# Who asks for which weight blocks: eight blocks of the last batch by SyncE instead of GpSimd, two blocks of the first routed task by GpSimd instead of SyncE

## The chip, the core and the metric

The kernel runs on one core of a Trainium2 chip. The core has TensorE (PE in the profile, with its weight loads as PEld), VectorE (DVE), ScalarE (ACT), GpSimd (POOL) and SyncE (SP), which run their own instruction queues and wait for each other by semaphores. Sixteen DMA engines move data between HBM and the on-chip memory SBUF; SyncE and ScalarE ask for plain transfers, GpSimd for gathers by a list of row numbers. The metric is the device time of one execution in microseconds (us), the median of several runs.

## What is computed

The reference chains three layers. Attention runs over 4 batches of 8 heads, 1152 keys and 576 pooled queries, and its 2304 output rows of 512 numbers go through a routed mixture of eight experts and then through a soft one:

```
x = attention(q, k, v)                  # 2304 rows of 512
logits = x @ w_gate + modality_bias[modality_id]
e_idx = argmax(logits, axis=1)
for e in range(8):
    mask = e_idx == e
    h = maximum(x[mask] @ w1[e], 0)     # 512 -> 1024
    out[mask] = gate_w[mask] * (h @ w2[e])
# third layer: 32 slots, softmax over rows, eight experts on four slots each
return (softmax(logits2, 1) @ slot_out)
```

Which rows go to which expert is known only while the kernel runs, so the weights of an expert are fetched by an index that the kernel has computed.

## The kernel before, in words

**Attention.** `attention` walks over 16 pairs (batch, two heads), p = 0 to 15. In each pair 36 positions follow each other; at a position TensorE makes scores (lines 266 and 272), ScalarE their exponentials (`e`, line 276), TensorE the product with V (line 286), VectorE the row maxima for the next pair (line 219) and GpSimd the sums of the exponentials (`acc`, lines 297 and 299). Other work is hung on positions by tables of numbers. In the middle pairs SyncE loads a later pair; from p = 13 on no pair is left to load.

**The task ahead.** At the end of batch 2 the kernel picks the expert with most rows so far (`Ahead.select`; its index list is `awidx`, line 1036, one column for each quarter of w1 and w2, row e x 128 + partition). A first task for this expert, the "task ahead", is prepared while the last batch is still in attention, in memory that attention no longer needs (`KX`, `QX`, one `V`). `Ahead.fetch(i)`, line 1047, brings its eight weight blocks of 128 x 1024 floats (512 KB): four of w1, then four of w2. Two are fetched in p = 13, four in p = 14, at positions 1, 5, 21 and 25, and two at the start of p = 15. `Ahead.split(u)` cuts half a block into a high and a low part (ScalarE line 796, VectorE line 797): blocks 0 to 2 during p = 14 and 3 to 5 during p = 15, the rest behind attention. `Ahead.load_x` gathers the task's 256 rows in p = 15.

**The routed tasks.** Behind attention `make_tasks` finds, on VectorE, which expert each of eight static tasks has (`widx`, line 758) and which rows (`xidx`, line 739). `ffn`, inside it `chain`, runs these tasks (t = 0 to 7, and a half task). Each has eight blocks; for t = 0 the order is (w1, quarter 0), (w2, 0), (w1, 1), (w2, 1), and so on. `fetch` in `chain` (line 1187) has SyncE read the expert's row number from `widx` into a register and then asks for a block at that address; since the rows of one quarter of one expert lie one behind the other, that is one plain transfer. Four buffers take the blocks (`RAWS`). At the start the loop of line 1214 asks for four blocks; ahead of block number `min(BX, NRAW - 1)`, which is 3, it puts `load_x(ts[0])`, the gather of task 0's 256 rows in two halves of 128 x 520 floats (`xg`, line 1109, by GpSimd through `gather`, line 775).

**The seam.** Behind that loop come, in program order, four splits (the fourth cuts the first half of block (w1, 1), the third one asked for), and `xT`: TensorE turns the rows (line 784, tile `tp`), ScalarE copies the high part (`xh`, line 791) and VectorE takes the low part (`xl`, line 792). TensorE does the last units of the task ahead (lines 819 to 821) in between. The first product of task 0 is line 805 (`xh`), the second line 806 (`xl`). Each engine keeps its program order, so what stands ahead of `xh` on ScalarE has to be done first.

Of the kernel before, what the change touches and what calls it, by code (L numbers as in the profile page):

```python
# [25 lines left out]
E = 8  # L26
# [51 lines left out]
OUTB = ((6, 6, 6), (8, 10), (2, 4, 4, 8))  # L78
NRAW = sum(RAWS)
BT = 6  # L80
BX = 3
BS = (1, 3)
NHI = 5
NH = 2
# [689 lines left out]
def gather(nc, out, src, idx):  # L774
    return nc.gpsimd.indirect_dma_start(out=out, out_offset=None, in_=src,  # L775
                                        in_offset=bass.IndirectOffsetOnAxis(ap=idx, axis=0))
# [18 lines left out]
def cut_parts(nc, hi, lo, x):  # L795
    nc.scalar.copy(hi, x)  # L796
    nc.vector.tensor_sub(lo, x, hi.bitcast(F32))  # L797


def ffn1(nc, g, wh, wl, xh, xl):  # L800

    hp = g["ps"].tile([128, 512], F32, name="hp", tag="sc", bufs=3)[:, :TS]
    for k in range(DM // 128):
        c = slice(k * 128, (k + 1) * 128)
        nc.tensor.matmul(hp, wh[:, c], xh[:, k], start=(k == 0), stop=False)  # L805
        nc.tensor.matmul(hp, wh[:, c], xl[:, k], start=False, stop=False)  # L806
        nc.tensor.matmul(hp, wl[:, c], xh[:, k], start=False, stop=(k == DM // 128 - 1))  # L807
    return hp


def relu_parts(nc, hp, hh, hl):
    nc.scalar.activation(hh, hp, AF.Relu)  # L812
    nc.vector.scalar_tensor_tensor(out=hl, in0=hp, scalar=0.0, in1=hh.bitcast(F32), op0=ALU.max, op1=ALU.subtract)  # L813


def ffn2(nc, yp, f, hh, hl, wh, wl):
    for h in range(2):
        hs = slice(h * 128, (h + 1) * 128)
        nc.tensor.matmul(yp[h], hh[:, hs], wh, start=(f == 0), stop=False)  # L819
        nc.tensor.matmul(yp[h], hh[:, hs], wl, start=False, stop=False)  # L820
        nc.tensor.matmul(yp[h], hl[:, hs], wh, start=False, stop=(f == F // 128 - 1))  # L821
# [159 lines left out]
class Ahead:  # L981
# [62 lines left out]
        ]  # L1044

    def fetch(self, i):
        gather(self.tc.nc, self.raw[i], self.g["w1" if i < 4 else "w2"], self.widx[:, i % 4:i % 4 + 1])

    def load_x(self, h):
        gather(self.tc.nc, self.xg[h], self.g["xs"][0:PAD + (B - 1) * SQ, :], self.xidx[:, h:h + 1])  # L1050
# [33 lines left out]
def ffn(ctx, tc, g):  # L1084
    nc = tc.nc
# [19 lines left out]
    def load_x(t, xg=None):  # L1105
        halves = 1 if t == HT else 2
        xg = xg or [xp1.tile([128, XW], F32, name=f"xg{h}") for h in range(halves)]
        for h in range(halves):
            gather(nc, xg[h], g["xs"], g["xidx"][:, h, t:t + 1])
        st[t] = dict(xg=xg, gt=xp.tile([128, 2], F32, name="gt"))  # L1110

    def xT(t):
        s = st[t]
        xh = xp1.tile([128, KD, TS], F32R, name="xh")
        xl = xp1.tile([128, KD, TS], F32R, name="xl")
        s["xh"], s["xl"] = xh, xl
        if t == HT:
            nc.gpsimd.tensor_copy(s["gt"][:, 0:1], s["xg"][0][:, DM:DM + 1])
            tp = ps.tile([128, KD, 128], F32, name="tp", tag="mx", bufs=3)
            for k in range(KD):  # L1120
                nc.tensor.transpose(tp[:, k], s["xg"][0][:, k * 128:(k + 1) * 128], ident)
            cut_parts(nc, xh[:, :, 0:128], xl[:, :, 0:128], tp)
            return
        for h in range(2):
            nc.gpsimd.tensor_copy(s["gt"][:, h:h + 1], s["xg"][h][:, DM:DM + 1])
        for a in range(KD // 2):
            k2 = slice(2 * a, 2 * a + 2)
            turn_rows(nc, g, s["xg"], a, xh[:, k2], xl[:, k2])
# [38 lines left out]
    def chain(ts, hooks, between=lambda: False):  # L1167

        seq = []
        for t in ts:  # L1170
            if t == HT:
                seq += [(t, w, f) for w, f0, n in ((1, 0, 4), (2, 0, 2), (1, 4, 2), (2, 2, 2), (1, 6, 2), (2, 4, 4)) for f in range(f0, f0 + n)]
                continue
            seq += [(t, 1, 0)] + [x for f in range(1, 8) for x in ((t, 1, f), (t, 2, f - 1))] + [(t, 2, 7)]
        pieces = sorted({(t, w, f // 2) for t, w, f in seq}, key=lambda x: seq.index((x[0], x[1], 2 * x[2])))
        raw, part, used, row = {}, {}, set(), {}
        left = [len(RAWS)]

        def fetch():
            if pieces:  # L1180
                t, w, q = pieces.pop(0)
                m = len(pieces) % NRAW
                i = next(i for i in range(len(RAWS)) if m < sum(RAWS[:i + 1]))
                raw[t, w, q] = raws[i].tile([128, 1024], F32, name="wraw", bufs=RAWS[i])
                if t not in row:
                    row[t] = nc.sync.value_load(g["widx"][0:1, 0, t:t + 1], min_val=0, max_val=(E - 1) * 128)
                nc.sync.dma_start(out=raw[t, w, q], in_=g[f"w{w}"][bass.ds(row[t] + q * E * 128, 128), :])

        def split(i):
            if i < len(seq):  # L1190
                t, w, f = seq[i]
                x = raw[t, w, f // 2]
                if (t, w) == (HT, 2):
                    part[t, w, f] = x, None
                    return
                part[t, w, f] = hi, lo = g["parts"]()
                if (t, w) == (HT, 1):
                    cut_parts(nc, four(hi), four(lo), x.rearrange("p (f k c) -> p f k c", f=2, k=KD)[:, :, f % 2 * 2:f % 2 * 2 + 2])
                else:
                    cut_parts(nc, hi, lo, x[:, (f % 2) * 512:(f % 2 + 1) * 512])  # L1200
                if f % 2:
                    done(t, w, f)

        def done(t, w, f):
            used.add((t, w, f // 2))
            while raw and next(iter(raw)) in used:
                raw.pop(next(iter(raw)))
                fetch()
                while left[0] and len(raw) <= sum(RAWS[:left[0] - 1]):
                    left[0] -= 1  # L1210
                    cs[left[0]].close()
                    open_more(NWR[left[0]])

        for i in range(NRAW):
            if i == min(BX, NRAW - 1):
                load_x(ts[0])
            fetch()
        for _ in range(BT):
            between()
        for i in range(NHI - 1):  # L1220
            split(i)
            if i in BS:
                between()
        xT(ts[0])
        while between():
            pass
        for i, (t, w, f) in enumerate(seq):
            s = st[t]
            nx = ts[ts.index(t) + 1] if t != ts[-1] else None
            hi, lo = part.pop((t, w, f))  # L1230
            if t == HT:
                half(s, w, f, hi, lo)
                if w == 2 and f % 2:
                    done(t, w, f)
                if (w, f) == (1, 0):
                    load_x(nx)
                if (w, f) == (1, 7):
                    xT(nx)
                if (w, f) == (2, 7):
                    todo.extend([None] + front.put([s["yp"]], s["gt"], [g["xidx"][:, 0, t:t + 1]], t))  # L1240
                    todo.extend(front.group())
                    st.pop(t)
            elif w == 1:
                hp = ffn1(nc, g, hi, lo, s["xh"], s["xl"])
                s["h", f] = [xp1.tile([128, TS], F32R, name=c, bufs=NH) for c in ("hh", "hl")]
                relu_parts(nc, hp, *s["h", f])
                if f == 0 and nx is not None:
                    load_x(nx)
                if f == 7 and nx is not None:
                    xT(nx)  # L1250
            else:
                if f == 0:
                    s["yp"] = [ps.tile([128, DM], F32, name="yp", tag="pv", bufs=2) for _ in range(2)]
                if (t, f) in hooks:
                    hooks[t, f]()
                ffn2(nc, s["yp"], f, *s.pop(("h", f)), hi, lo)
                if f == 7:
                    todo.extend([None] + front.put(s["yp"], s["gt"], [g["xidx"][:, h, t:t + 1] for h in range(2)], t, nx is None))
                    if t in (0, 2, 5, NSTAT - 1):
                        todo.extend(front.group(nx is None))  # L1260
                    st.pop(t)
            step()
            split(i + NHI - 1)
# [13 lines left out]
    def between():  # L1277
        if g["rest"]:
            g["rest"].pop(0)()
            return True  # L1280
        if "open" in g:
            g.pop("open")()
        return False
# [11 lines left out]
    def open_more(n):  # L1295
        if n:
            g["ws"].add(g["right"](f"s_wr{len(g['ws'].tiles)}", n), n)
        while g["prefetch"]():
            pass
# [524 lines left out]
```

## Time and profile before

| | us |
|---|---|
| median of three runs | 804.16 |
| lowest and highest of them | 801.02, 805.23 |
| the profiled execution, its own time | 802.14 |
| span of the profiled execution | 800.3 |

| engine | busy us | share of the span |
|---|---|---|
| PE | 779.0 | 97% |
| DVE | 561.4 | 70% |
| POOL | 470.5 | 59% |
| ACT | 463.2 | 58% |

All times of the trace count from the start of the span. Attention ends at about 488 us, the seam lies between 488 and 521 us, the routed tasks run to about 740 us and the soft mixture follows. A line of a timeline gives the start, the duration, the engine, the line of the kernel, the operation with its output and inputs, how many there are, and in square brackets the idle time of the engine ahead of it with what ended that. The profile's list of DMA issues gives the time from the issue to the landing.

### The profile page before, as it was taken

How to read it: one execution, taken by the hardware profiler on the slowest of the kernel's cores; microseconds unless marked ns; L12 is line 12 of the kernel's file. 1: busy time of each engine (PE TensorE's matmuls, PEld its weight loads, DVE VectorE, ACT ScalarE, POOL GpSimd, SP SyncE). 2: the span in 40 equal slices, each digit the busy share in tenths (PEclk: the TensorE clock that was granted, in tenths of full speed). 3: DMA queues.
4: the chain of work that ended last, by engine and by line, in shares of the span. 5: the costliest groups of instructions: out<-in, count | busy, mean ns of one | idle time of the engine just before them, and what ended most of it. 6: DMA issues, size and time to landing. Idle time of an engine off the chain costs nothing.

```text
span 800.3 us, 16064 instructions
## 1 busy us (share of the span) xinstructions
PE 779.0 (97%) x5696; PEld 597.1 (75%) x5696; DVE 561.4 (70%) x1168; ACT 463.2 (58%) x1100; POOL 470.5 (59%) x429
## 2 busy tenths in 40 slices
PE   5999999999999999999999999999999999999997
PEld 4767777777777677777666667798898789988466
DVE  7768777769777878776878786766666566665272
ACT  5555665656776657776556964355554555554232
POOL 6978899999988987878978963311402211020200
PEclk9999999999999999999999999999999999999999
DMA  9797558674665584755564220677777787976997
GB/s 323 183 271 193 125 160 223 158 216 135 154 175 149 137 225 149 179 141 145 121 151 126 78 81 2 218 260 253 270 265 226 256 288 264 339 269 230 377 386 240
DMA packets 55608, 162.83 MB, mean 203 GB/s; under 512 B 12138, under 2 KB 19610, under 8 KB 51418
## 3 DMA queue, kind: packets, MB, share of 16 engines
q1 hardware_dynamic: 49652, 134.76, 56.3%
q10 hardware_dynamic: 2592, 17.43, 5.9%
q0 software_dynamic: 3280, 9.57, 3.9%
q8 instruction: 47, 0.77, 0.4%
q14 instruction: 37, 0.30, 0.1%
HBM read 110.45 MB, written 10.89 MB: 152 GB/s over the span
## 4 chain that ended last, share of the span: by engine, by line
PE 88%; DVE 5%; ACT 2%; DMA 2%; POOL 1%; issue 1%; ACTq 0%; POOLq 0%
PE pv L286 18%; PE sc L266 12%; PE sc L272 9%; PE mps L217 8%; PE hp L805 4%; PE hp L807 4%; PE hp L806 4%; PE yp L819 4%; PE yp L821 4%; PE yp L820 4%; PE sg L319 2%; PE hp L1551 2%; DVE mxp L219 2%; PE tp L346 2%; PE op L1566 1%; PE tp L784 1%
## 5 line engine op out<-in xcount | busy, mean ns | idle before, releaser
L299 POOL TENSOR_TENSOR acc<-acc,e 128x576 f32<-128x576 f32 x214 | 316.9, 1481 | 20.3 <-ACT e L276 6.8
L276 ACT ACTIVATE e<-sc 128x288 f32<-128x288 f32 x576 | 224.8, 410 | 131.2 <-PE sc L272 111.6
L219 DVE TENSOR_REDUCE mxp<-mps 128x1 f32<-128x384 f32 x432 | 220.3, 549 | 92.3 <-PE mps L217 85.5
L266 PE MATMUL sc<-QS,KS 128*128 128x288 f32 x576 | 185.4, 330 | 1.2 <-ACT e L276 1.0
L272 PE MATMUL sc<-QL,KH 69*128 69x288 f32 x576 | 169.7, 297 | 0.4 <-ACT QB L537 0.3
L286 PE MATMUL pv<-e,V 128*64 128x288 f32 x1152 | 160.9, 415 | 0.0
L266 PEld LDWEIGHTS sc<-QS,KS 128*128 128x128 f32 x576 | 108.9, 189 | 52.9 <-issue 21.0
L217 PE MATMUL mps<-KS,QS 128*128 128x384 f32 x384 | 134.6, 354 | 9.7 <-ACT QS L487 7.3
L286 PEld LDWEIGHTS pv<-e,V 128*64 128x64 f32 x1152 | 74.2, 136 | 60.5 <-issue 22.3
L272 PEld LDWEIGHTS sc<-QL,KH 69*128 69x128 f32 x576 | 108.9, 189 | 0.8 <-POOL qs L486 0.5
L797 DVE TENSOR_TENSOR wlo<-wraw,whi 128x512 fp32r<-128x512 f32 x136 | 90.0, 687 | 21.8 <-ACT whi L796 19.3
L796 ACT CAST whi<-wraw 128x512 fp32r<-128x512 f32 x136 | 79.1, 619 | 9.6 <-DMA wraw<-in_w 5.4
L217 PEld LDWEIGHTS mps<-KS,QS 128*128 128x128 f32 x384 | 73.8, 193 | 14.4 <-ACT QS L487 7.7
L805 PE MATMUL hp<-xh,whi 128*128 128x256 f32 x256 | 73.3, 286 | 0.0
L807 PE MATMUL hp<-xh,wlo 128*128 128x256 f32 x256 | 71.6, 280 | 0.0
L806 PE MATMUL hp<-xl,whi 128*128 128x256 f32 x256 | 71.5, 279 | 0.0
L962 POOL DMA_INDIRECT ls<-both,xidx x17 | 18.0, 1057 | 88.7 <-DVE both L944 45.5
L812 ACT ACTIVATE hh<-hp 128x256 fp32r<-128x256 f32 x64 | 24.5, 383 | 78.4 <-PE hp L807 76.2
L775 POOL DMA_INDIRECT xg<-xs,xidx x17 | 19.0, 1119 | 85.1 <-PE tp L784 52.1
L297 POOL TENSOR_TENSOR acc<-e 128x576 f32<-128x576 f32 x31 | 44.6, 1439 | 32.3 <-ACT e L276 32.2
L813 DVE SCALAR_TENSOR_TENSOR hl<-hp,hh 128x256 fp32r<-128x256 f32 x64 | 27.2, 424 | 45.7 <-ACT hh L812 45.7
L819 PE MATMUL yp<-whi,hh 128*128 128x512 f32 x128 | 52.9, 413 | 0.1
(412 smaller groups left out, 1242.3 us busy)
## 6 DMA issues: line engine op xcount, KB each, us to landing
wraw<-in_w SPq DMA_DIRECT2D x72, 512.0 KB, 4.5
mw<-in_m2w ACTq DMA_DIRECT2D x16, 1024.0 KB, 5.7
mw<-in_m2w SPq DMA_DIRECT2D x16, 1024.0 KB, 8.0
V<-in_vT SPq DMA_DIRECT2D x16, 576.0 KB, 3.8
KX<-in_kT SPq DMA_DIRECT2D x15, 576.0 KB, 4.4
QX<-in_qT SPq DMA_DIRECT2D x15, 576.0 KB, 5.1
KS<-KC SPq DMA_DIRECT2D x30, 288.0 KB, 4.1
QS<-QC SPq DMA_DIRECT2D x60, 144.0 KB, 3.8
```

The costliest lines, as they stand in the source:

```text
L217: nc.tensor.matmul(mps[:, :384], s["QS"][:, j, blk * 128:(blk + 1) * 128], s["KS"][:, j, ks], start=True, stop=True)
L219: V.reduce_max(s["mxp"][:, slot, t:t + 1], mps[:, :384], axis=AX.X)
L266: nc.tensor.matmul(sc[:, :NU], s["KS"][:, j, c * 128:(c + 1) * 128], s["QS"][:, j, u * NU:(u + 1) * NU], start=True, stop=False)
L272: nc.tensor.matmul(sc[:, :NU], s["KH"][0:69, j, c * 128:(c + 1) * 128], s["QL"][0:69, j, u * NU:(u + 1) * NU], start=False, stop=True)
L276: nc.scalar.activation(s["e", u, c][:, j], sc[:, :NU], AF.Exp, scale=SM)
L286: nc.tensor.matmul(pv[j * 64:(j + 1) * 64, :NU], s["v"][:, j, c, :], e[:, j], start=(c == 0), stop=(c == NKB - 1))
L299: eng.tensor_add(s["acc", u], s["acc", u], s["e", u, c])
L797: nc.vector.tensor_sub(lo, x, hi.bitcast(F32))
L805: nc.tensor.matmul(hp, wh[:, c], xh[:, k], start=(k == 0), stop=False)
L806: nc.tensor.matmul(hp, wh[:, c], xl[:, k], start=False, stop=False)
L807: nc.tensor.matmul(hp, wl[:, c], xh[:, k], start=False, stop=(k == DM // 128 - 1))
L819: nc.tensor.matmul(yp[h], hh[:, hs], wh, start=(f == 0), stop=False)
```

## The change

`Ahead.fetch` asks for a block by SyncE. At block 0 SyncE reads the expert's row number from `awidx` into a register, which all eight blocks use. `BX` goes from 3 to 2, so that task 0's rows are asked for behind two blocks, and for task 0 the blocks of quarter 1, the third and the fourth, are asked for by GpSimd with a gather instead of by SyncE.

```
-BX = 3
+BX = 2
...
     def fetch(self, i):
-        gather(self.tc.nc, self.raw[i], self.g["w1" if i < 4 else "w2"], self.widx[:, i % 4:i % 4 + 1])
+        nc = self.tc.nc
+        if i == 0:
+            self.row = nc.sync.value_load(self.widx[0:1, 0:1], min_val=0, max_val=(E - 1) * 128)
+        nc.sync.dma_start(out=self.raw[i], in_=self.g["w1" if i < 4 else "w2"][bass.ds(self.row + i % 4 * E * 128, 128), :])
...
                 raw[t, w, q] = raws[i].tile([128, 1024], F32, name="wraw", bufs=RAWS[i])
+                if (t, q) == (0, 1):
+                    gather(nc, raw[t, w, q], g[f"w{w}"], g["widx"][:, q, t:t + 1])
+                    return
                 if t not in row:
```

TensorE, ScalarE and VectorE have the same instructions in the same order as before; GpSimd has ten rows fewer in its list, eight gathers gone and two added, with the sums now in longer runs.

On GpSimd, from p = 13 to p = 15, this stood in a row before (`acc` are the sums of exponentials, `KX`, `QX` and `V_162` the blocks of the task ahead, `V_161` its rows):

```order
184 L775 DMA KX_151<-in_w,awidx 128x1024
185 L775 DMA QX_153<-in_w,awidx 128x1024
186 L299 TENSOR_TENSOR acc<-acc,e 128x576 x3
187 L775 DMA KX_152<-in_w,awidx 128x1024
188 L299 TENSOR_TENSOR acc<-acc,e 128x576 x3
189 L775 DMA QX_154<-in_w,awidx 128x1024
190 L297 TENSOR_TENSOR acc<-e 128x576
191 L299 TENSOR_TENSOR acc<-acc,e 128x576 x7
192 L775 DMA V_162<-in_w,awidx 128x1024
193 L775 DMA KX_151<-in_w,awidx 128x1024
```

and on SyncE of the changed kernel the eight requests stand here, behind the last operand copies of attention (line 155) and ahead of the store of the last batch's rows (line 433):

```order
176 L155 DMA QL_148<-QLc 64x576 x2
177 L1049 TENSOR_LOAD awidx
178 L1049 ISA x2
179 L1050 ISA
180 L1050 DMA KX_151<-in_w 128x1024
181 L1050 ISA
182 L1050 DMA QX_153<-in_w 128x1024
...
194 L1050 DMA KX_152<-in_w 128x1024
195 L433 DMA xs<-xr 96x6x520
196 L1192 TENSOR_LOAD widx
```

The gathers have left the sums of GpSimd, and the requests stand one behind the other on SyncE, where nothing stood between the lines 155 and 433.

At the seam GpSimd had the rows of task 0 and then their gate column (`gt`, line 1125):

```order
205 L391 TENSOR_SCALAR rA<-i_108,rdf,tok 96x72 x3
206 L775 DMA xg_6881<-xs,xidx 128x520
207 L775 DMA xg_6882<-xs,xidx 128x520
208 L1125 COPY gt<-xg_6881 128x1
209 L1125 COPY gt<-xg_6882 128x1
```

and the changed kernel has there:

```order
194 L391 TENSOR_SCALAR rA<-i_108,rdf,tok 96x72 x3
195 L775 DMA xg_6888<-xs,xidx 128x520
196 L775 DMA xg_6889<-xs,xidx 128x520
197 L775 DMA wraw<-in_w,widx 128x1024 x2
198 L1128 COPY gt<-xg_6888 128x1
199 L1128 COPY gt<-xg_6889 128x1
```

Two blocks of weights have come in behind the rows; on SyncE the first run of blocks is two requests shorter.

## Rows read from the trace of the kernel before

**Rows 1.** The page, part 1: busy us, share, instructions.

```profile
PE 779.0 (97%) x5696; PEld 597.1 (75%) x5696; DVE 561.4 (70%) x1168; ACT 463.2 (58%) x1100; POOL 470.5 (59%) x429
```

**Rows 2.** Busy time by stretch, p = 12 and p = 14: us, PE, PEld, DVE, ACT, POOL.

```profile
370.70:399.10 28.40, 28.40 (x195) 20.31 (x195) 21.87 (x47) 17.52 (x45) 26.16 (x20) 1.00 0.48 117
...
431.40:462.20 30.80, 29.63 (x200) 20.42 (x198) 24.73 (x48) 26.57 (x71) 28.99 (x21) 1.00 0.23 69
```

**Rows 3.** Waits of PE from 399 to 520 us: total, times, longest.

```profile
PE tp L784 <- DMA xg<-xs,xidx: 1.1, 1, 1.1
PE sc L266 <- ACT e L276: 1.0, 2, 0.8
```

**Rows 4.** Groups of POOL from 424 to 466 us: busy, mean ns, idle before.

```profile
L775 POOL DMA_INDIRECT KX<-in_w,awidx x4 | 4.1, 1020 | 2.2 <-DVE awidx L1036 1.4 <-DVE mxp L219 0.3 <-issue 0.3
L775 POOL DMA_INDIRECT QX<-in_w,awidx x3 | 2.9, 957 | 0.6 <-ACT e L276 0.3 <-issue 0.2
...
L775 POOL DMA_INDIRECT V<-in_w,awidx x1 | 1.0, 957 | 0.1
```

**Rows 5.** Waits of all engines from 431 to 462 us, the longest.

```profile
ACT e L276 <- PE sc L272: 2.8, 5, 0.9
```

**Rows 6.** Timeline of SyncE's issues, 412 to 530 us.

```profile
421.01 1.92 SPq L155 DMA_DIRECT2D QL<-QLc  x2
501.62 0.32 SPq L433 DMA_DIRECT2D xs<-xr  x1
507.88 22.01 SPq L1187 DMA_DIRECT2D wraw<-in_w  x8
```

**Rows 7.** Timeline of DVE: the two index lists.

```profile
424.36 0.15 DVE L1036 SCALAR_TENSOR_TENSOR awidx<-aex,pioq 128x4 int32<-128x4 f32 x1
...
506.45 0.23 DVE L758 SCALAR_TENSOR_TENSOR widx<-exi,pioq 128x72 int32<-128x72 f32 x1
```

**Rows 8.** Timeline of POOL, 511 to 523 us: gathers of rows.

```profile
511.65 1.07 POOL L775 DMA_INDIRECT xg<-xs,xidx  x1 [7.99 <-PE bp L740]
513.02 2.74 POOL L775 DMA_INDIRECT xg<-xs,xidx  x1 [0.30 <-issue]
...
520.10 0.97 POOL L775 DMA_INDIRECT xg<-xs,xidx  x1 [1.41 <-PE tp L784]
```

**Rows 9.** DMA issues at 507.9, 509.5, 513.0, 520.1, 426.4, 464.0 us: KB, landing.

```profile
wraw<-in_w SPq DMA_DIRECT2D x1, 512.0 KB, 3.5
...
wraw<-in_w SPq DMA_DIRECT2D x1, 512.0 KB, 6.5
...
xg<-xs,xidx POOLq DMA_INDIRECT x1, 5.4
...
xg<-xs,xidx POOLq DMA_INDIRECT x1, 3.2
...
QX<-in_w,awidx POOLq DMA_INDIRECT x1, 4.9
...
KX<-in_w,awidx POOLq DMA_INDIRECT x1, 6.2
```

**Rows 10.** Timeline of ACT, 517 to 520 us.

```profile
517.31 0.62 ACT L796 CAST whi<-wraw 128x512 fp32r<-128x512 f32 x1 [0.78 <-PE yp L821]
519.06 1.08 ACT L791 CAST xh<-tp 128x512 fp32r<-128x512 f32 x2 [1.14 <-PE tp L784]
```

**Rows 11.** Timeline of DVE, 517 to 521 us.

```profile
517.96 0.69 DVE L797 TENSOR_TENSOR wlo<-wraw,whi 128x512 fp32r<-128x512 f32 x1 [0.70 <-ACT whi L796]
519.68 1.29 DVE L792 TENSOR_TENSOR xl<-tp,xh 128x512 fp32r<-128x512 f32 x2 [1.03 <-ACT xh L791]
```

**Rows 12.** Timeline of PE, 517 to 521 us.

```profile
518.48 0.99 PE L784 MATMUL tp<-ident,xg 128*128 128x128 f32 x7 [1.10 <-DMA xg<-xs,xidx]
...
520.70 0.28 PE L805 MATMUL hp<-xh,whi 128*128 128x256 f32 x1
520.81 0.28 PE L806 MATMUL hp<-xl,whi 128*128 128x256 f32 x1
```

## The prediction, made before the changed kernel ran

> **What bounds the kernel now.** I read the page first: TensorE is busy in 97% of the span [rows 1], so a change pays only where TensorE waits, or where what it does is late. Then I read the busy time by attention pair and TensorE's waits up to the seam, since the change touches 424 to 466 us (the eight blocks of the task ahead) and 508 to 521 us (the first blocks of task 0). In p = 14, where four of the eight gathers sit, the pair takes 30.8 us against 28.4 in p = 12, and TensorE idles 30.8 - 29.6 = 1.2 us of it [rows 2]. What rises there is ScalarE, 26.6 us busy against 17.5; GpSimd is busy 29.0 us against 26.2, nearly all of the time, but the waits of that stretch put nothing at its door: ScalarE waits most for scores of TensorE, 2.8 us [rows 5], and the 1.0 us that TensorE waits for exponentials between 399 and 520 us [rows 3] is ScalarE's own queue. At the seam TensorE waits once, 1.1 us for the rows of task 0 [rows 3]. These two waits, 2.1 us together, are nearly all that the change can touch.
>
> **Part A, the eight blocks.** Eight gathers leave GpSimd: 4.1 + 2.9 + 1.0 = 8.0 us busy, with 2.9 us of gaps ahead of them [rows 4], so some 11 us of GpSimd's 42. Who waits for GpSimd there? The sums of the exponentials follow behind, their buffers go back to ScalarE, and TensorE uses a finished sum twice in a pair. No wait of the stretch ends on a sum; the longest is the one quoted [rows 5]. So the 11 us are cover, not path, and I cost them at nothing. The bounds: at most the whole excess of p = 14 over p = 12, 30.8 - 28.4 = 2.4 us [rows 2], if GpSimd were its hidden cause; on the other side, sums that now start earlier lie beside other instructions of VectorE, which share their stretch with them, and I allow as a loss what TensorE waits for VectorE or ScalarE at one such place, 1.0 us [rows 3]. I take zero because the excess is ScalarE's, whose instructions do not change.
>
> What the blocks gain as a new home: SyncE issues its last operand copy at 421.0 + 1.9 = 422.9 us and nothing more until 501.6 [rows 6]. The register read waits for `awidx`, done at 424.5 [rows 7]; in the later place of the same form 507.88 - (506.45 + 0.23) = 1.2 us lie between the list and the first issue [rows 6, 7], so the first block goes out at about 425.7 instead of 424.8. The blocks behind wait in SyncE's order for VectorE to be done with the old content of the buffers, at the latest at the cut of block 2 in p = 14; queued behind them is only the store of line 433, which waits until 501.6 anyway. So several transfers start earlier, none has a reader earlier, and no other transfer stands behind them. Cost nothing; if that cover failed, it would be ScalarE at its cut that waited.
>
> **Part B, the start of task 0.** Before, SyncE had asked for four blocks by 509.8 us, and they took 3.5 us (the first) to 6.5 us (the fourth) to land [rows 9]. The gather of the rows starts at 511.65 [rows 8], because the last product on the row table has just ended; that does not move, for `BX` moves a position in SyncE's and GpSimd's common program order, not what the gather waits for. But the rows meet two blocks instead of four. The second half then landed 5.4 us after its issue; the next gather of rows, with no such crowd, took 3.2 [rows 9]. So the rows land at 513.02 + 3.2 = 516.2 instead of 518.4, ahead of the time when TensorE asks for them (518.48 - 1.10 = 517.4), and the wait of 1.1 us [rows 12] goes. TensorE then reaches the first product of task 0 at 520.70 - 1.10 = 519.6.
>
> What is late next is the third block. Its cut is the fourth split, and on ScalarE it stands ahead of `xh`: it ran at 517.31 and `xh` at 519.06 [rows 10]; on VectorE the low part of the cut stands ahead of `xl` likewise, 517.96 and 519.68 [rows 11]. Now GpSimd asks for this block behind both halves of the rows. I place it: second half of the rows at 513.02, 0.97 us for the instruction as in the later gather instead of the 2.74 seen in the crowd [rows 8], a gap of 0.30, so 514.3. The landing: a gathered block close behind another took 4.9 us at 426.4 and 6.2 at 464.0 [rows 9]; here two halves of rows go ahead, so 4.9 is the nearest, and the block is there at 519.2. Then ScalarE cuts in 0.62 us, VectorE takes the low part at +0.65 (517.96 - 517.31) with `xl` about 0.60 behind it, and half of the 1.29 us of `xl` [rows 10, 11] gives the first low rows: 0.65 + 0.60 + 0.65 = 1.9 us behind the landing. The second product of task 0, line 806, needs them and can start at 519.2 + 1.9 = 521.1; before it started at 520.81 [rows 12]. So the 1.1 us are won and 1.4 us are lost again in a new wait: +0.3 us.
>
> Bounds: with a landing in the 3.5 us of an uncrowded SyncE block [rows 9] the block is there at 517.8, `xl` at 519.7, and the gain is the whole 1.1 us; with 2.74 us for the second gather of rows as before and a landing of 6.2, it is 513.02 + 2.74 + 0.30 + 6.2 = 522.3, `xl` at 524.2, a loss of 3.4 us. TensorE is the engine that is busy throughout [rows 1], so I count what is lost or won here as staying to the end. The fourth block is asked for 1.3 us behind the third; its first cut is the seventh split, which comes behind the first three units of task 0, so it has more room than the third and I cost it at nothing.
>
> The Trainium skill (DMA: Bandwidth & Descriptors, section "Issuing engine by pattern") leaves plain loads to SyncE and says that its path is generally the faster one. That speaks for the eight blocks and against the two. Its fit for a transfer issued by GpSimd (section "Anatomy of one DMA"), 2.0 us plus bytes over 436 GB/s, makes 3.2 us for 512 KB, as an estimate. The rows show 4.9 and 6.2 us for a block behind another, so the measurement decides; by the fit the block would be there at 517.5 and the change worth the whole 1.1 us.
>
> **The sum.** A 0.0, B +0.3: the profiled execution's 802.1 us becomes 802.4. The three runs have 801.0, 804.2 and 805.2, so that execution lies 2.0 us under their median; the four have a mean of 803.1, which I take as the level of the kernel before. Forecast 803.1 + 0.3 = 803.4 us, no change that can be told: 0.5% is 4.0 us, about what a measurement of this kernel can tell from no change.
>
> **The rivals.**
>
> Slower: the third block is late. The second gather of rows still takes 2.74 us, because the crowd is not what stretched it (the first took 1.07 us in the same crowd [rows 8]), and the block starts at 516.06 and lands at 521.0 to 522.3. ScalarE and VectorE stand at the cut, `xh` and `xl` behind it, TensorE at line 806. It costs from a landing at 518.9 on, and here 2.1 to 3.4 us: 805.9 with 2.8. For it speaks that nothing explains the 2.74; against it that the gather of rows at 520.1, with no crowd, took 0.97.
>
> Faster: GpSimd was the hidden cause of p = 14. Without gathers between them the sums keep up, buffers come back earlier and the pair falls to the 28.4 us of p = 12: -2.4 + 0.3, 801.0. For it speaks that GpSimd is busy 29.0 of 30.8 us [rows 2]; against it that nobody waits for it by the trace.
>
> Faster by the seam: the third block lands as early as one of SyncE's, and the whole wait of 1.1 us is gone: 802.0.
>
> Nothing moves: a wait that I have not seen, for a buffer or for a transfer counted on the same semaphore, holds the rows to their old landing and the blocks with them: 803.1.
>
> **How the numbers follow.** Forecast 0.60; slower by the third block 0.17; faster by GpSimd 0.11; faster by the seam 0.08; nothing moves 0.04. The likeliest stays at 803.4. None of the cases reaches 4.0 us by itself; only with the spread of single executions, 801.0 to 805.2, can a median cross it, mostly from the first and second rival: faster by over 0.5% 0.06, within 0.5% 0.88, slower 0.06. The range takes in the faster rival at 801.0 and the middle of the slower one at 805.9, with a little of the spread on top: 800.9 to 806.4.
>
> **What will show it.** Right: no gather of a block on GpSimd from 424 to 466 us, and p = 14 still near 30.8 us with ScalarE at 26.6; TensorE's wait for the rows gone; the cast of the third block on ScalarE waiting for a DMA until about 519.2; line 806 at 521.1 instead of 520.8 (both moved by what p = 13 to 15 gain). The second gather of rows at 0.97 us shows that the crowd had stretched it. Wrong: p = 14 shorter by over a microsecond, which makes GpSimd the cause; the cast waiting beyond 520.5, which makes the third block the loss; any wait of ScalarE at the cuts of the task ahead, which would say that SyncE's order holds those blocks back.

## The result, and the profile after

The changed kernel takes 808.05 us (median of six runs, 807.31 to 809.12) beside 803.99 us for the kernel before (six runs, 801.02 to 805.23): a ratio of 1.0058, 95% interval 1.0041 to 1.0074. By the medians it is slower by 4.1 us; the ratio stands for 4.7. The forecast of 803.4 us and its range up to 806.4 are both missed.

The page, part 1, of the changed kernel (busy us, share, instructions), against [rows 1]: GpSimd has lost 9 us of work and VectorE 4, and nothing else has moved by over 2.

```profile
PE 780.9 (97%) x5696; PEld 598.3 (74%) x5696; DVE 557.7 (69%) x1168; ACT 462.7 (57%) x1100; POOL 461.4 (57%) x423
```

**Part A came out as forecast.** SyncE's issues in the changed kernel: the eight blocks stand at line 1050; the first and the last are shown. This profiled execution runs 2.95 us behind the one of before at the seam, nearly all of it from the first 40 us, ahead of anything that the change touches; so 428.96 here is 426.0 there, and the prediction said 425.7. (Three dots mark lines left out, here and below.)

```profile
428.96 0.37 SPq L1050 DMA_DIRECT2D KX<-in_w  x1
...
463.47 0.33 SPq L1050 DMA_DIRECT2D KX<-in_w  x1
```

Busy time of p = 14, as in the second line of [rows 2], 2.95 us later (us, PE, PEld, DVE, ACT, POOL). ScalarE is at 26.7, as before, and the pair is as long as before: ScalarE's rows of lines 289 and 324 from p = 13 to p = 15 all come 2.94 to 3.13 us later than in the kernel before. And that although GpSimd is busy for 23.7 us instead of 29.0. GpSimd was not the hidden cause.

```profile
434.35:465.15 30.80, 29.69 (x200) 20.53 (x198) 22.27 (x48) 26.71 (x71) 23.65 (x17) 1.00 0.24 75
```

**The seam did not.** Waits of TensorE from 400 to 527 us, against [rows 3]: the wait for the rows is not gone but longer, and two new ones stand behind it, at the first and second product of task 0 (total, times, longest).

```profile
PE hp L805 <- ACT xh L791: 1.7, 1, 1.7
PE tp L784 <- DMA xg<-xs,xidx: 1.6, 1, 1.6
...
PE hp L806 <- DVE xl L792: 0.5, 1, 0.5
```

GpSimd's timeline at the seam, against [rows 8]: the second gather of the rows takes 2.74 us as before, and only then come the two blocks.

```profile
514.60 1.07 POOL L775 DMA_INDIRECT xg<-xs,xidx  x1 [7.97 <-PE bp L740]
515.98 2.74 POOL L775 DMA_INDIRECT xg<-xs,xidx  x1 [0.30 <-issue]
519.02 0.95 POOL L775 DMA_INDIRECT wraw<-in_w,widx  x1 [0.30 <-issue]
520.27 0.94 POOL L775 DMA_INDIRECT wraw<-in_w,widx  x1 [0.30 <-issue]
```

ScalarE's timeline, against [rows 10]: the cast of the third block waits 5.44 us for its transfer, and `xh` stands behind it.

```profile
524.92 0.62 ACT L796 CAST whi<-wraw 128x512 fp32r<-128x512 f32 x1 [5.44 <-DMA wraw<-in_w,widx]
525.44 1.06 ACT L791 CAST xh<-tp 128x512 fp32r<-128x512 f32 x2
```

TensorE's timeline, against [rows 12]:

```profile
526.07 0.38 PE L805 MATMUL hp<-xh,whi 128*128 128x256 f32 x1 [1.74 <-ACT xh L791]
526.91 0.39 PE L806 MATMUL hp<-xl,whi 128*128 128x256 f32 x1 [0.46 <-DVE xl L792]
```

Since the executions are shifted against each other, I measure the seam from the row list on: from the start of `xidx` on VectorE (line 739) to the start of line 806 on TensorE. Before that is 520.81 - 510.62 = 10.19 us, in the changed kernel 526.91 - 513.57 = 13.34. The seam has become 3.15 us longer. Behind line 806 both profiled executions need the same time to the end, 279.5 and 279.1 us.

VectorE's timelines show what stood beside the two second gathers, first before, then after:

```profile
510.62 0.20 DVE L739 TENSOR_TENSOR xidx<-bp,zt 128x36 int32<-128x36 f32 x1
511.51 0.41 DVE L741 TENSOR_SCALAR both<-bp 18x256 f32<-18x256 f32 x1 [0.70 <-PE bp L740]
511.86 1.27 DVE L797 TENSOR_TENSOR wlo<-QX,whi 128x512 fp32r<-128x512 f32 x2
513.06 1.27 DVE L797 TENSOR_TENSOR wlo<-KX,whi 128x512 fp32r<-128x512 f32 x2
514.26 0.67 DVE L797 TENSOR_TENSOR wlo<-wraw,whi 128x512 fp32r<-128x512 f32 x1
515.16 0.69 DVE L797 TENSOR_TENSOR wlo<-wraw,whi 128x512 fp32r<-128x512 f32 x1 [0.22 <-ACT whi L796]
```

```profile
513.57 0.20 DVE L739 TENSOR_TENSOR xidx<-bp,zt 128x36 int32<-128x36 f32 x1
...
514.81 1.27 DVE L797 TENSOR_TENSOR wlo<-QX,whi 128x512 fp32r<-128x512 f32 x2
516.01 1.28 DVE L797 TENSOR_TENSOR wlo<-KX,whi 128x512 fp32r<-128x512 f32 x2
517.22 0.67 DVE L797 TENSOR_TENSOR wlo<-wraw,whi 128x512 fp32r<-128x512 f32 x1
```

Five subtractions, each with two operands in SBUF, follow each other without a pause. Before, the last of them ends at 514.93 and the gather at 513.02 + 2.74 = 515.76; after, at 517.89 and at 518.72. Both times the gather ends 0.83 us behind the string, nearly the whole 0.94 to 0.97 us of the gathers above with no such string beside them. From this comes the theory of the experiments: **while such a string runs, GpSimd's gather stands still.** The Trainium skill (SBUF — State Buffer, section "SBUF: two separate sides") says that VectorE, for an operation with two inputs in SBUF, and a GpSimd operation that reads SBUF share a pair of ports as an exclusive lock, and that the one that starts later stands still for the whole instruction of the other. The rows above agree in that the gather, which has its row list in SBUF, stands still; but it does so for the whole string, past the ends of four instructions. How long it lasts, and whether the start decides, is measured below.

### The profile page after: what moved, and what is told of

It is laid out like the page before. It is cut to its first block, busy times and chain, and to the rows that moved or that the text cites. A ratio compares the mean times of both kernels' runs of the same rounds, so it can differ in the third digit from the quotient of the medians.

```text
span 806.0 us, 16072 instructions
## 1 busy us (share of the span) xinstructions
PE 780.9 (97%) x5696; PEld 598.3 (74%) x5696; DVE 557.7 (69%) x1168; ACT 462.7 (57%) x1100; POOL 461.4 (57%) x423
## 4 chain that ended last, share of the span: by engine, by line
PE 87%; DVE 7%; ACT 2%; POOL 1%; DMA 1%; issue 1%; ACTq 0%; POOLq 0%
PE pv L286 18%; PE sc L266 12%; PE sc L272 9%; PE mps L217 8%; PE hp L805 4%; PE hp L806 4%; PE hp L807 4%; PE yp L819 4%; PE yp L821 4%; PE yp L820 4%; DVE mxp L219 2%; PE sg L319 2%; PE hp L1557 2%; PE tp L346 2%; PE op L1572 1%; PE tp L853 1%
```

## The experiments

"Distance" is the one from the row list to line 806; a time is a ratio to runs of the kernel before made beside it, with its 95% interval. Between the two ends of the distance TensorE has the same 41 products in every kernel, those on constants in kernel 12 apart. Lengths and distances are those of one profiled execution each.

| kernel | gathers of the rows, us | third block: gather to cast, us | distance, us | ratio |
|---|---|---|---|---|
| before | 1.07, 2.74 | | 10.19 | |
| changed | 1.07, 2.74 | 5.90 | 13.34 | 1.0058 [1.0041, 1.0074] |
| 1: part A alone | 1.07, 2.73 | | 10.17 | 1.0005 [0.9986, 1.0023] |
| 2: part B alone | 1.07, 2.73 | 5.76 | 13.21 | 1.0071 [1.0048, 1.0094] |
| 3: fourth block only | 1.08, 2.73 | | 10.15 | 0.9993 [0.9979, 1.0008] |
| 4: third block only | 1.07, 2.73 | 5.43 | 12.88 | 1.0043 [1.0029, 1.0058] |
| 5: third block ahead of the rows | 0.95, 2.85 | | 10.19 | 0.9997 [0.9984, 1.0010] |
| 6: four of the five subtractions left out | 1.07, 0.95 | 5.10 | 10.76 | 1.0028 [1.0015, 1.0042] |
| 7: memsets between them | 1.07, 2.78 | | 10.09 | 1.0006 [0.9991, 1.0020] |
| 8: low parts in both pauses | 3.03, 0.95 | | 12.72 | 1.0017 [1.0002, 1.0032] |
| 9: low part in the first pause | 2.43, 0.95 | | 9.84 | 1.0006 [0.9994, 1.0019] |
| 10: the same, in the changed kernel | 2.43, 0.95 | 5.42 | 12.43 | 1.0057 [1.0038, 1.0076] |
| 11: low parts early | 1.31, 0.95 | | 8.87 | 0.9970 [0.9955, 0.9985] |
| 12: changed, TensorE kept busy | 1.08, 2.73 | 5.68 | 13.56 | 1.0027 [1.0009, 1.0044] |

### 1 and 2: the two parts apart

Kernel 1 is the kernel before with the new `Ahead.fetch`, kernel 2 the changed kernel with the old one.

> The kernel before with the first part of the change alone: the eight blocks of the last batch's task ahead are asked for by SyncE from a register's address, the first routed task's blocks stay as they were. If the whole loss of the change is made by the third block at the seam, this kernel is within 0.5 us of the kernel before (the trace of after shows ScalarE's offset about 0.4 us smaller behind the fifteenth pass than ahead of the thirteenth), the second rows' gather takes 2.74 us again and the four blocks are asked for and land as before. If on the other hand SyncE's register load and its eight blocks carry the loss (by late blocks in the thirteenth to fifteenth passes, or by a clock that falls), this kernel is 3 to 4 us slower than the kernel before, near 808, and the next kernel is near 804.

> The kernel before with the second part of the change alone: the first routed task's third and fourth block asked for by GpSimd behind its rows, the blocks of the task ahead still gathered. If the third block's late landing is the whole loss: 3 to 4 us slower than the kernel before, 807 to 808.5, with the second rows' gather at 2.74 us, the third block's gather starting only when that ends, its landing some 5.8 us after its start, and TensorE waiting at the hidden products (hp) for the split of that block by 1.7 and 0.5 us as in the profile of after. If the loss needs both parts together, this one is under 1.5 us slower.

Part A is worth nothing that can be measured, and part B carries the whole loss: with it alone the distance is 13.21 us, and TensorE waits 2.1 and 0.5 us at lines 805 and 806:

```profile
522.74 0.38 PE L805 MATMUL hp<-xh,whi 128*128 128x256 f32 x1 [2.10 <-ACT xh L791]
523.58 0.58 PE L806 MATMUL hp<-xl,whi 128*128 128x256 f32 x1 [0.46 <-DVE xl L792]
```

### 3 and 4: which of the two blocks

Against the changed kernel, in kernel 3:

```
-                if (t, q) == (0, 1):
+                if (t, w, q) == (0, 2, 1):
```

In kernel 4 it is (0, 1, 1).

> The changed kernel with the third block given back to SyncE: only the fourth block (second quarter of w2) is asked for by GpSimd behind the rows. Theory 'the third block is the loss': the cast of the third block on ScalarE no longer waits for a transfer, TensorE reaches the first product of task 0 as early as in the kernel before, and the time is that of the kernel before within 1 us (803 to 805). Theory 'both blocks are late': the seventh split waits for the fourth block, TensorE stands behind the third unit of task 0, and 2 us or more of the loss stay (806 or more). The second gather of the rows is expected at 2.7 us again, since VectorE's subtractions are unchanged.

> The changed kernel with the fourth block given back to SyncE: only the third block (second quarter of w1) is asked for by GpSimd behind the rows. Theory 'the third block is the loss': 3 to 4.5 us slower than the kernel before (807 to 808.5), with the cast of the third block waiting for its transfer. If the block landed 5.8 us after its gather because the fourth block was gathered right behind it and shared the transfer engines, it lands here within 5 us and the loss falls by 0.8 us or more; if the rows ahead of it in GpSimd's queue set that, it is 5.8 us again. The fourth block of SyncE, issued earlier, should be there long before its split.

ScalarE's cast of the third block, in kernel 3 and in kernel 4:

```profile
519.45 0.62 ACT L796 CAST whi<-wraw 128x512 fp32r<-128x512 f32 x1 [0.78 <-PE yp L821]
```

```profile
521.74 0.62 ACT L796 CAST whi<-wraw 128x512 fp32r<-128x512 f32 x1 [4.98 <-DMA wraw<-in_w,widx]
```

In kernel 3 it waits for TensorE, as before, and no time is lost: the fourth block has the room that the prediction gave it. In kernel 4 it waits for the transfer. The third block makes the loss. From its gather to its cast it takes 5.43 us instead of 5.90, where I had expected 0.8 us less if the fourth block slowed it. That the fourth block makes this 0.5 us is not shown: kernel 10 has both blocks and takes 5.42 us as well, kernel 6 has both and takes 5.10. What else differs is SyncE's next request, task 0's fifth block. It goes out 0.2 us ahead of the third block's gather in the changed kernel (518.83) and in kernels 2, 4 and 12 (5.4 to 5.9 us), and 1.6 us behind it in kernels 6 and 10 (5.1 and 5.4 us). Kernels 6 and 10 have the same order here and differ by 0.3 us, so these runs do not tell the two apart.

### 5: GpSimd asks, but ahead of the rows

The changed kernel with the old place of the rows:

```
-BX = 2
+BX = 3
```

> The changed kernel with BX left at 3: GpSimd asks for the third block ahead of the rows and for the fourth behind them. The list of the block is ready at about 506.7 us, some 5 us before the rows' gather can start, and GpSimd stands idle then. Theory 'what costs is the place behind the rows, not that GpSimd asks': the third block lands by 513 us, its cast on ScalarE waits for no transfer, and the time is within 1 us of the kernel before (803 to 805). Theory 'a gathered block costs by itself' (its path is slower, or it holds up the rows): TensorE still waits at the first products of task 0 by over a microsecond, 805.5 or more.

GpSimd's gather of the third block, and ScalarE's cast of it:

```profile
510.39 1.12 POOL L775 DMA_INDIRECT wraw<-in_w,widx  x1 [3.86 <-DMA xs<-xr]
```

```profile
520.17 0.62 ACT L796 CAST whi<-wraw 128x512 fp32r<-128x512 f32 x1 [0.78 <-PE yp L821]
```

Nothing is lost. That GpSimd asks costs nothing; the place behind two gathers of rows, one of them held, does.

### 6: what holds the second gather

In the changed kernel, in `Ahead.split`; it leaves out the low parts of the last four half blocks of the task ahead, for which ScalarE writes zeros:

```
+        if u >= 12:
+            x = self.raw[u // 2][:, (u % 2) * 512:(u % 2 + 1) * 512]
+            self.tc.nc.scalar.copy(self.hi[u], x)
+            self.tc.nc.scalar.mul(self.lo[u], x, 0.0)
+            return
```

> The changed kernel without VectorE's subtractions in the last four half blocks of the task ahead: ScalarE writes zeros there instead, so that the low part of these four half blocks of w2 is left out of the computation. Those subtractions, with two inputs in SBUF, run back to back on VectorE exactly while the second rows' gather lasts 2.74 us. Theory 'VectorE holds GpSimd': the second rows' gather takes 0.9 to 1.3 us, the third block's gather starts 1.4 to 1.8 us earlier, its block lands that much earlier, and the time falls by 1.4 to 1.8 us against the changed kernel (806.2 to 806.7). Theory 'GpSimd's second gather in a row is long by itself' or by the transfers then in flight: it stays at 2.74 us, and the time stays within 0.5 us of 808.

GpSimd's timeline, and VectorE's at the same place:

```profile
513.36 0.95 POOL L775 DMA_INDIRECT xg<-xs,xidx  x1 [0.30 <-issue]
514.61 0.94 POOL L775 DMA_INDIRECT wraw<-in_w,widx  x1 [0.30 <-issue]
515.86 1.19 POOL L775 DMA_INDIRECT wraw<-in_w,widx  x1 [0.31 <-issue]
```

```profile
513.54 0.69 DVE L797 TENSOR_TENSOR wlo<-wraw,whi 128x512 fp32r<-128x512 f32 x1 [1.28 <-ACT whi L796]
515.54 0.69 DVE L797 TENSOR_TENSOR wlo<-wraw,whi 128x512 fp32r<-128x512 f32 x1 [1.31 <-ACT whi L796]
```

The second gather falls from 2.74 to 0.95 us: VectorE's string is the cause, not the transfers in flight. The distance falls by 2.6 us, 1.8 of them by the gather and 0.8 by the landing of the third block, 5.10 us instead of 5.90. The gather of the fourth block shows it on a small scale: it starts at 515.86 within a single subtraction, 515.54 to 516.23, and ends at 517.05, 0.82 us behind it. The second gather of the rows, which starts 0.18 us ahead of a single subtraction, is not held. The distance is 0.57 us above that of the kernel before; the time is above it by 1.2 to 3.4 us, more than the seam accounts for, so that this kernel does not give the size of the seam's loss from its time alone.

### 7: a small instruction between the subtractions

In the kernel before, in `Ahead.split`:

```
+        if u >= 12:
+            self.tc.nc.vector.memset(self.g["lastnm"], 0.0)
```

> The kernel before with one small extra instruction on VectorE, a memset of a column, ahead of each of those four subtractions; nothing else changes. Theory 'VectorE holds GpSimd': between two subtractions GpSimd gets in, so the second rows' gather (2.74 us in the kernel before) falls to 0.9 to 1.6 us, the second half of the rows lands 1.1 to 1.8 us earlier, TensorE's wait of 1.1 us at the first transposition of the rows' second half goes, and the time falls by 0 to 1.1 us (802.9 to 804). Theory 'long by itself or by the transfers': 2.74 us again, the wait of 1.1 us stands, and the time is that of the kernel before within 0.3 us.

```profile
512.78 2.78 POOL L775 DMA_INDIRECT xg<-xs,xidx  x1 [0.30 <-issue]
```

```profile
512.84 0.68 DVE L797 TENSOR_TENSOR wlo<-KX,whi 128x512 fp32r<-128x512 f32 x1
512.85 0.06 DVE L1065 MEMSET lastnm<- 128x1 f32 x1
...
514.06 0.67 DVE L797 TENSOR_TENSOR wlo<-wraw,whi 128x512 fp32r<-128x512 f32 x1
```

This was meant to let GpSimd in and did not: the memsets leave no gap (the next subtraction starts 0.61 us behind the last as before), and the gather again ends 0.83 us behind the end of the string, 514.73. By the letter of the expectation this outcome speaks for the other theory, a gather that is long by itself; kernels 6 and 11 rule that out. A memset that leaves no gap is no pause.

### 8, 9 and 10: the subtractions moved

The task ahead's half blocks 12 to 15 are cut by `cut(12)` to `cut(15)`. The first order puts two low parts into VectorE's pauses ahead of and behind `xidx` (`cut(12)`, `cut(13)`), and `cut(15)` behind task 0's second split; the second fills only the first pause, and defers the low parts of `cut(15)` and of task 0's first split behind the second split. Kernel 10 is the changed kernel with that second order.

The first lines of the edit in short (the second one in kernel 8 alone):

```
+        cut(12)
         V.scalar_tensor_tensor(out=zt, ...
         V.tensor_add(g["xidx"], b3, zt)
+        cut(13)
```

> The kernel before with the order of VectorE's subtractions at the seam changed and nothing else: the first two of the four low parts of the task ahead run in VectorE's two pauses of 0.7 us ahead of and behind the row list, the fourth behind the second cut of task 0, so that none of them is in progress when the second gather of the rows starts at 513.0 us. Theory 'a gather that starts while VectorE subtracts two operands in SBUF ends only 0.8 us after that string of subtractions ends': the second gather falls from 2.74 to 0.9 to 1.0 us, the second half of the rows lands 1.0 to 1.8 us earlier, TensorE's wait of 1.1 us at the transposition goes, and the time falls by 0.7 to 1.1 us (802.5 to 803.3 where the kernel before is at 803.6). Theory 'long by itself': 2.74 us, the wait stands, and the time moves by under 0.3 us.

> The kernel before with VectorE's order at the seam changed in another way: the first low part of the task ahead runs in VectorE's pause ahead of the row list, the second and third behind it, and the fourth and the first cut of task 0 only behind task 0's second cut, which waits for ScalarE. So no subtraction stands just ahead of the first gather, and the string that is in progress when the second gather starts at 513.0 us ends at 513.1 and is followed by a pause. Theory 'a gather gets on only when VectorE's unbroken string with such subtractions ends, and then needs 0.8 us more': the first gather takes 1.1 us, the second 0.9 to 1.1, the second half of the rows lands about 1.8 us earlier, TensorE's wait of 1.1 us at the transposition goes, and the time falls by 0.7 to 1.1 us. Theory 'one of the two gathers is always long': one of them takes 2.7 us or more again, as where the pause behind the list was filled as well (3.03 us for the first), and the wait stays at 1 us or more.

> The changed kernel, complete, with the same order of VectorE at the seam: both parts of the change, and the second gather of the rows free. This is what the prediction assumed of the gather (0.97 us). Theory 'two mis-sized terms, the gather and the block's landing': the third block's gather starts 1.7 us earlier than in the changed kernel, it lands 5.0 to 5.9 us later, not 4.9, TensorE reaches the second product of task 0 about 1.0 to 1.5 us later than in the kernel before, and the time is 1 to 2 us over the kernel before (804.5 to 805.5), against 4.4 for the changed kernel. Theory 'the gather was the only mis-sized term': within 0.5 us of the kernel before.

GpSimd's gathers of the rows in kernel 8, and in kernel 9 with VectorE's subtractions there:

```profile
513.79 3.03 POOL L778 DMA_INDIRECT xg<-xs,xidx  x1 [7.98 <-PE bp L743]
517.13 0.95 POOL L778 DMA_INDIRECT xg<-xs,xidx  x1 [0.30 <-issue]
```

```profile
513.33 2.43 POOL L778 DMA_INDIRECT xg<-xs,xidx  x1 [7.97 <-PE bp L743]
516.07 0.95 POOL L778 DMA_INDIRECT xg<-xs,xidx  x1 [0.30 <-issue]
```

```profile
513.54 0.67 DVE L803 TENSOR_TENSOR wlo<-QX,whi 128x512 fp32r<-128x512 f32 x1
514.14 0.67 DVE L803 TENSOR_TENSOR wlo<-KX,whi 128x512 fp32r<-128x512 f32 x1
```

The second gather is free in all three, and the first is held instead; in kernel 9 it ends at 515.76, 0.95 us behind the string's end at 514.81. So none gave what was expected: kernel 8 came out 0.2% slower instead of 0.1% faster (TensorE waits 1.9 us for the rows, and its products from there to line 806 run at a granted clock of 0.55 to 0.59, from 522 to 526 us, so that part of the 12.72 us is the clock's), kernel 9 kept a wait of 0.8 us, and kernel 10 asked for the third block only 0.4 us earlier than the changed kernel and lost as much as that. The expectation took the first gather to be safe, since no subtraction stood just ahead of it. In kernel 9 it starts 0.21 us ahead of the string, as in the kernel before, and is held all the same; in the kernel before it is not.

### 11: the string moved ahead of the gathers

The kernel before again, with the second order of VectorE but three low parts ahead of line 740, in short:

```
+        cut(12)
         V.scalar_tensor_tensor(out=zt, ...
         V.tensor_add(g["xidx"], b3, zt)
+        cut(13)
+        cut(14)
         nc.tensor.matmul(bp[:NT, 256:512], sel, g["tabs"], start=True, stop=True)
```

The low parts of `cut(15)` and of the first split of task 0 are deferred as in kernel 9.

> The kernel before with VectorE's order at the seam changed in a third way: the first low part of the task ahead ahead of the row list, the second and third right behind it and ahead of the line that waits for TensorE's row table, the fourth and the first cut of task 0 behind task 0's second cut. The string of subtractions then ends at about 512.0 us, 0.4 us behind the start of the rows' first gather, and VectorE pauses until 515.2. Theory 'a gather gets on when VectorE's string ends and needs 0.8 to 0.95 us more': the first gather ends by 513.4, the second takes 0.95 and ends by 514.7, 1.0 to 1.8 us earlier than in the kernel before; TensorE's wait for the rows falls from 1.1 us to 0.3 or less, from the row list to the second product of task 0 it is 9.2 to 9.5 us instead of 10.2, and the time falls by 0.7 to 1.0 us, which five rounds can hardly tell. Theory 'one of the two is always held for 1.5 to 2 us': the distance stays at 9.8 us or more.

GpSimd's gathers and VectorE's last lines ahead of its pause:

```profile
514.26 1.31 POOL L780 DMA_INDIRECT xg<-xs,xidx  x1 [7.98 <-PE bp L745]
515.88 0.95 POOL L780 DMA_INDIRECT xg<-xs,xidx  x1 [0.30 <-issue]
```

```profile
513.94 0.69 DVE L805 TENSOR_TENSOR wlo<-KX,whi 128x512 fp32r<-128x512 f32 x1
514.54 0.41 DVE L746 TENSOR_SCALAR both<-bp 18x256 f32<-18x256 f32 x1
```

The string ends at 514.63 and the first gather 0.94 us later, although VectorE goes on with line 746, which reads PSUM: that operation does not hold it. The second gather ends 3.60 us behind the start of `xidx` instead of 5.14, TensorE's wait for the rows is gone, the distance is 8.87 us, 1.3 less than before, and the time is 802.2 us beside 804.2, a ratio of 0.9970. This version beats both kernels.

### 12: TensorE's clock behind the seam

The distance has grown by 3.15 us and the time by 4.1, in kernel 2 by 3.0 and 4.7. In kernel 2 the rows show where more was lost. Busy time of a stretch, with the granted clock behind POOL's time, and the same product of task 0 in that stretch and behind it:

```profile
522.00:530.00 8.00, 6.80 (x39) 6.29 (x39) 4.55 (x8) 4.63 (x10) 0.49 (x3) 0.79 0.31 91
```

```profile
524.18 0.42 PE L805 MATMUL hp<-xh,whi 128*128 128x256 f32 x1
...
527.06 0.28 PE L805 MATMUL hp<-xh,whi 128*128 128x256 f32 x1
```

Behind its waits of 1.1, 2.1 and 0.5 us TensorE runs a stretch at a granted clock of 0.50 (524 to 526 us), the 1.2 GHz level, before it is back at 2.4: a product takes 0.42 instead of 0.28 us and starts 0.21 instead of 0.12 us behind the last. From line 806 to the next transpositions (line 853) kernel 2 takes 4.19 us, the kernel before 2.61: 1.6 us for the clock in this execution. Such a stretch stands in the profiled executions of kernels 2, 4 and 10 right behind the seam and in that of kernel 8 at its end; their waits at the seam come to 1.9 to 3.7 us. The executions whose waits there come to 1.5 us or less have none. Nor has the changed kernel's own, with 3.8 us (it has one at 38 us, part of the 3 us named above). But its six runs have a mean granted clock of 0.995 to 0.998, 0.9963 on average; 29 runs of the kernel before, made beside kernels 1 and 2, average 0.9989. The Trainium skill (TensorE: Matmul & The Clock Gate, section "What's actually happening") has a gate at these two levels that follows how busy TensorE has been; the rows of these four agree, the changed kernel's, at 1.00 behind 3.8 us of waits, do not show it.

The test keeps TensorE busy in its waits, with products on constants:

```
+        warm = ps.tile([128, 512], F32, name="warm", tag="sc", bufs=3)
+        warm_up(nc, g, warm, 9)
         xT(ts[0])
         while between():
             pass
+        warm_up(nc, g, warm, 12)
```

> The changed kernel with idle work for TensorE in its two waits at the seam: 9 small products on constants ahead of the transpositions of the rows and 12 ahead of the first product of task 0, whose results nobody reads; they take about as long as the waits. The seam itself is not shorter: from the row list to the second product of task 0 it stays at 13.2 to 13.6 us against 10.2 in the kernel before. Theory 'the rest of the loss is TensorE's clock, which falls behind a seam with long waits': the mean granted clock of the runs rises from 0.996 to 0.998 or more, near the 0.999 of the kernel before, and the time falls by 1 to 1.7 us to 806.3 to 807, which leaves the 3.1 us of the seam. Theory 'the clock has no part in it': the time stays within 0.5 us of 808.

```profile
521.00:529.00 8.00, 8.00 (x63) 7.61 (x62) 4.09 (x7) 4.21 (x9) 2.30 (x4) 1.00 0.45 148
```

The distance stays at 13.56 us, the mean granted clock of the twelve runs rises to 0.9988, that of the kernel before beside them (0.9987), and the time falls to 806.6 us beside 804.2. So a part of the changed kernel's loss is the clock's: 1.6 us by the medians (4.1 against 2.4 us over the kernel before), 2.5 by the ratios (0.6 to 4.4, estimated from their intervals).

## Why the prediction was wrong

**Part A, zero: right.** The first block, p = 14 and ScalarE's share came out as forecast, and kernel 1 has a ratio of 1.0005. The rival with GpSimd as hidden cause is refuted by p = 14: 5 us less work on GpSimd, and the pair as long as before.

**"0.97 us for the instruction as in the later gather instead of the 2.74 seen in the crowd": wrong, and the step that decided.** The crowd of four blocks did not stretch the second gather. With two blocks it took 2.74 us again; without the subtractions beside it 0.95 (kernel 6). Rows were at hand for doubt: the first gather had taken 1.07 us in the same crowd, and the rival said so. The prediction did not ask which engine was busy from 513.0 to 515.8 us: VectorE's string ended 0.83 us ahead of the gather's end. From this wrong step two errors came: the rows did not land earlier (TensorE got the second half 5.97 us behind its issue, not 3.2, so the wait of 1.1 us did not go: it is 1.6 here and 1.1 in kernel 2; where the 0.5 comes from stays open), and the third block was asked for 1.77 us late.

**"The landing: 4.9 is the nearest": too low by 1.0 us.** From its gather to its cast the third block took 5.9 us, short of the upper bound of 6.2. The prediction counted only the two halves of rows ahead of it and left out task 0's fifth block, which SyncE asks for 0.2 us ahead, and the fourth block behind it; how much of the 1.0 is whose stays open (kernels 4, 6 and 10). The sum, mended in these two terms: the forecast for line 806 was 521.1; 521.1 + 1.77 + 1.0 = 523.9, and measured is 526.91 - 2.95 = 523.96. The mechanism, ScalarE and VectorE at the cut with `xh` and `xl` behind it, was right; the sizes were not. The rest of the miss in the time is the level, 803.1 taken for a kernel whose six runs have a median of 804.0, and the clock: 803.4 + 0.9 + 2.8 = 807.1, which leaves 1 us of the 808.05.

**The rival "the third block is late" is what happened**, by the mechanism that it named, at the upper end of its 2.1 to 3.4 us: 3.15. It had a chance of 0.17, and its time of 805.9 is still too low.

**"What is lost or won here stays to the end": short by the clock.** The 3.15 us stayed, and about 1 us came on top by the medians. Kernel 12 puts 1.6 to 2.5 us, uncertain by some 2, on the clock, which falls to 1.2 GHz behind such waits in four traces. No term of the sum had a price for the clock, since the kernel before keeps 1.00 through its seam.

**The fourth block, at nothing: right** for its own readers (kernel 3); whether it delays the third block stays open.

## What to carry to other kernels

Ahead of moving work behind an instruction that once took longer than its like, find out what made it long: look at what every other engine did in those microseconds, not only at the transfers. A gather by GpSimd belongs where VectorE pauses or reads PSUM, not into a string of operations with two inputs in SBUF, and a block that someone waits for belongs ahead of gathers whose list comes later (kernel 5), not behind them. A wait of TensorE costs more than itself when its clock falls behind it.

## What was not expected of the hardware

- A gather of 128 rows with no such string beside it takes 0.94 to 0.98 us on GpSimd in most rows here. Where one was held by VectorE's subtractions of two SBUF operands, it ended 0.82 to 0.96 us behind the end of the string, in the kernel before, the changed kernel and kernels 6 to 11, so hardly any of it was done while they ran. A memset between them did not let it in (kernel 7); an operation on PSUM behind them did (kernel 11).
- Which comes first is not decided by the starts in the profile. In the kernel before the first gather starts 0.21 us ahead of the string and is not held; in kernel 9 it starts as much ahead and is. Nor is the string always closed: in kernel 10 the third block's gather starts at 515.96 within the first of four subtractions without a pause and takes 1.03 us. What decides stays open, and so the theory above holds for the held gathers only.
- In kernels 2, 4, 8 and 10 the granted clock fell at the seam behind waits of TensorE of 1.9 to 3.7 us in all, none of them longer than 2.1 us, with products in between; in the changed kernel's trace it did not, behind 3.8 us.
